# Moving a router's gate logits to VectorE and cutting expert units to 64 rows

## The chip, the cores and the metric

The kernel runs on one core of a Trainium2 chip. The metric is the time of one execution in device microseconds (us). A core has TensorE (PE, with PEld for its weight loads), VectorE (DVE), ScalarE (ACT), GpSimd (POOL) and SyncE (SP, which here only issues DMAs). Each engine works through its own list of instructions in order. It waits for the others by semaphores.

## The reference

Three layers follow each other. B = 2, H = 8, S = 768, D = 64, so there are 1536 tokens of 512 channels.

```python
scores = where(is_sink | in_window, q @ k.T / 8, -1e9)     # 4 sinks, window 128
x = softmax(scores) @ v                                     # attention
h = x @ w_in;  x = maximum(0.01 * h, h) @ w_out             # 512 -> 2048 -> 512, fp64 weights in
logits = x @ w_gate                                         # 512 -> 8 experts
expert = argmax(logits); gate = softmax(logits)[expert]
# each expert takes its first 384 tokens, the others' rows stay zero
out[token] = gate * (maximum(X[expert] @ w1[expert], 0) @ w2[expert])   # 512 -> 1024 -> 512
```

Of the 1536 tokens the experts 0 to 7 get 177, 257, 53, 101, 45, 4, 228 and 671 (the last is cut to 384).

## The kernel before

**Precision.** Every operand of a matmul is held as a high and a low part, and a product is the sum of three matmuls: high by high, high by low, low by high.

**Dense layers.** The tokens go in six blocks (j = 0 to 5) of 256, which is two tiles of 128 tokens. A block has 16 steps f, one for each 128 hidden channels. A step issues `first` (L1099, 12 matmuls of 256 columns into `hps`), a slice of the attention of later tiles, and the `second` of two steps before (L1147, 6 matmuls of 512 columns into `y`). Between the two lies the leaky ReLU: ACT L1117, DVE L1118 (`g`), and the split into `gp`. There are two `hps` buffers, so the `first` of step f+2 waits for the DVE `g` of step f. In block 0 the fp64 weights are also turned into fp32 by bit operations on VectorE ("words", L1010 to L1030), split into parts (`wl` on POOL, L1046) and stored. Later blocks read them from memory.

**Routing.** The router works on block j during block j+1. ACT L1224 copies the block's two `y` out as `x2`. `transpose` (L1233) turns them on TensorE by eight transposes (`xps`), and VectorE copies them out (`x2T`, L1235). `parts` (L1245, `kls`) and `logits` (L1258, `lps`) are ten small matmuls. Then come `place` (softmax, position in the expert's queue) and `scatter` (rows to the queues in memory). One of these calls is taken at each step of the tuple `ROUTE`.

**Experts.** `Experts` works through the experts by falling size, in seats: 0 to 3 are long (`group`), 4 is of one unit (`lone`), and 5 to 7 are of 64 rows (`half`). A unit is 128 rows. Seats 0 to 3 hold 384, 228, 177 and 257 rows, in the order 384, 228, 177, 257, thus 3, 2, 2 and 3 units. `group` first transposes the units after the first (L1617), working at the first ones' matmuls between (`up`, L1636, of one unit's 128 columns). Then the remaining matmuls of `up` run over all of the seat's columns, into four tiles `ph`. `h_parts` makes `ht` of them. `down` (L1685) takes 24 matmuls of 512 columns for each unit, and `out` scales and stores. In `half`, the high and low parts of 64 rows stand side by side in 128 columns, so that two matmuls do what three do elsewhere. The expert weights come by DMA as fp64 (`craw`), and ACT L1472 and DVE L1470 and L1474 make parts (`cw`) of them.

**Which path.** The number of units of each seat is known only when the counts are. The tuple `USUAL` names the expected numbers. If the counts agree, a path written out for them is run, and otherwise a general one with branches.

Of the kernel before, what the change touches and what calls it, by code (L numbers as in the profile page):

```python
# [18 lines left out]
P = 128  # L19
# [28 lines left out]
WORD_US = 0.6  # L48
PARTS_US = 2.0
ROUTE = (2, 4, 6, 9, 10, 11, 14)  # L50
HOLD, TAIL = 4, 1
# [377 lines left out]
class RingAttention(Attention):  # L429
# [298 lines left out]
    def pv_low(self, t, g):  # L728
        if (t, g) in self.lo:
            lo, hi, ps = self.lo.pop((t, g))  # L730
            self.pace.vector(0.4)
            self.nc.vector.tensor_tensor(out=lo, in0=ps, in1=hi.bitcast(F32), op=ALU.subtract)
# [218 lines left out]
class FFN:  # L951
# [198 lines left out]
class Router:  # L1150


    def __init__(self, nc, tc, pools, A, capacity, ident):
# [25 lines left out]
        self.lT = {}  # L1179
        nc.sync.dma_start(out=self.wg, in_=A["moe2_w_gate"].rearrange("(k p) e -> p k e", p=P))  # L1180

        self.before = c.tile([P, P], BF16, name="before")
# [45 lines left out]
    def transpose(self, ts):  # L1228
        nc = self.nc
        for t in ts:  # L1230
# [5 lines left out]
            self.xT[t] = xT  # L1236

    def parts(self, ts):

# [11 lines left out]
    def logits(self, ts):  # L1251
        nc, E, sm = self.nc, self.E, self.p["sm"]
        nt = len(ts)
        ps = self.p["ps"].tile([P, nt, E], F32, tag="att", name="lps")
        lT = self.lT.pop(ts, None)
        for n, t in enumerate(ts):
            if lT is not None:
# [123 lines left out]
class Experts:  # L1381
# [14 lines left out]
    PARTS = 50  # L1396
    USUAL = (3, 2, 2, 3)

    def __init__(self, nc, tc, pools, A, router, ident):
# [21 lines left out]
        self.tail = [gi for gi, (e, js) in enumerate(self.groups) if e >= self.short]  # L1421
        self.usual = self.USUAL if self.tail[0] == len(self.USUAL) == self.short else ()
        if self.usual:
            self.bounds = [self.p["const"].tile([P, self.short], F32, name=f"bound{a}") for a in range(2)]
            for (e, js), u in zip(self.groups, self.usual):
                nc.gpsimd.memset(self.bounds[0][:, e:e + 1], float((u - 1) * P + 1))
                nc.gpsimd.memset(self.bounds[1][:, e:e + 1], float(u * P if u < len(js) else 2 ** 20))

# [154 lines left out]
    def fetch(self, gi, n=0):  # L1583
# [4 lines left out]
        if gi < len(self.known):  # L1588
            for u in range(n, self.known[gi]):
                self.get(gi, u)  # L1590
            return
# [3 lines left out]
        if n < len(js):  # L1595
            with self.tc.If(self.csp[s] > js[n] * P):
                self.get(gi, n)
                if n + 1 < len(js):
                    self.fetch(gi, n + 1)

    def fetch_one(self, gi):
# [16 lines left out]

    def x_parts(self, gi, n, px):

        nc, DM = self.nc, self.DM
        h, l = (self.xt[:, a, :, n * P:(n + 1) * P] for a in range(2))
# [4 lines left out]
    def up(self, e, h, f, u0, u1):  # L1627

        nc = self.nc
        sl = slice(u0 * P, u1 * P)  # L1630
        mm = [(k, w, a) for k in range(self.K) for w, a in ((0, 0), (0, 1), (1, 0))]
# [7 lines left out]

    def h_parts(self, h, f, u, n):  # L1640

        nc = self.nc
        ps = self.ph[f][:, u * P:n * P]
        hh, hl = (self.ht[:, a, h * self.HF + f, u * P:n * P] for a in range(2))
        nc.scalar.activation(hh, ps, AF.Relu)
        nc.vector.scalar_tensor_tensor(out=hl, in0=ps, scalar=0.0, in1=hh.bitcast(F32), op0=ALU.max,
                                       op1=ALU.subtract)
# [27 lines left out]
    def down(self, e, h, n, turn=False, last=None):  # L1675
        nc = self.nc
        for f in range(self.HF):
# [6 lines left out]
            for m, (x, w) in enumerate(((hh, wh), (hh, wl), (hl, wh))):  # L1684
                nc.tensor.matmul(self.py[n], lhsT=x, rhs=w, start=(h == 0 and f == 0 and m == 0),  # L1685
                                 stop=(h == self.NH - 1 and f == self.HF - 1 and m == 2))

    def out(self, gi, n):
# [73 lines left out]

    def half_out(self, gi):
        nc, Q = self.nc, P // 2
        gt, ys, py = self.gt[gi % 4][0], self.ys[self.nout % 2], self.py[gi % 2]
        self.nout += 1
# [13 lines left out]
    def half(self, gi):  # L1780
# [22 lines left out]
        self.half_out(gi)  # L1803

    def group(self, gi, n, u0):

# [4 lines left out]
        nxt = gi + 1 < len(self.groups)  # L1811
        m = n - u0
        for u in range(u0 + (u0 == 0), n):
            px = self.px if (u - u0) % 2 == 0 else self.ph[3].rearrange("p (k c) -> p k c", k=self.K)
            if gi or u >= self.ready:
# [20 lines left out]
        for u in range(u0, n):  # L1836
            for h in range(self.NH):
                self.down(e, h, u)
                if u == n - 1:
                    self.release("b", gi, h)  # L1840
                    if h < self.NH - 1:
                        self.refill(self.PACE[2])
            self.out(gi, u)
        for h in range(0 if m > 0 else self.NH):
# [23 lines left out]
    def run(self):  # L1868
# [64 lines left out]
        with self.tc.If(self.off <= 0, preferred_fallthrough_block=True) as c:  # L1933
            self.known = self.usual + (1,) * len(tail)
            for gi, n in enumerate(self.usual):
                self.group(gi, n, int(gi == 0))
            self.known = ()
# [7 lines left out]
def build(tc, A, n_sink, window, capacity):  # L1945
# [14 lines left out]
    with ExitStack() as es:  # L1960
# [145 lines left out]

        pending, held, routing, splits = [], [], [], []
        n_ev = ffn.NF - ffn.CAP
        late = NB - 1

        def route(ts, ahead=False):
            return [lambda: rt.transpose(ts), *[lambda: rt.parts(ts)] * (ahead and rt.tiled), lambda: rt.logits(ts),
                    *[lambda: None] * (ahead and not rt.tiled), lambda: rt.place(ts),
                    *(lambda t=t: rt.scatter(t) for t in ts)]

        def split(n, f=-1, x=0):
# [5 lines left out]
        def second():  # L2122
# [23 lines left out]
            if last:  # L2146
                ts = tuple(range(j * TPB, (j + 1) * TPB))
                for t, y in zip(ts, ffn.y.pop(j)):
                    rt.evac(t, y)
                routing.extend(route(ts, True))  # L2150
                if j == late - 2 and rt.NU:
# [62 lines left out]
        rawst.close()  # L2214
        pool(es, "rt", bufs=2)
        for j in range(1, NB):
            need_t = TPB * (j + 2) - 1
# [3 lines left out]
            if j == late:  # L2221
                att.close()
# [113 lines left out]
```

## Time and profile before

| | |
|---|---|
| time, median of three executions | 570.53 us (570.47 to 570.69) |
| the profiled execution's own time | 570.18 us |
| its span, first to last instruction | 568.1 us |
| TensorE clock granted, mean | 0.998 |
| PE busy | 550.2 us (97%) |
| DVE busy | 341.0 us (60%) |
| ACT busy | 291.6 us (51%) |
| POOL busy | 186.4 us (33%) |
| DMA | 91.63 MB, mean 161 GB/s |

The span is 2.1 us shorter than the time of the same execution, since it leaves out what lies before the first and after the last instruction. An engine's share is an average over the whole span. The dense blocks 1 to 5 lie between about 100 and 395 us, the long seats between 400 and 517 us, and the short ones after them.

### The profile page before, as it was taken

The numbers are of one execution on the slowest core, as the hardware profiler recorded it, in microseconds if no ns is written. First come the engines' busy times: TensorE is split into PE (matmuls) and PEld (weight loads), VectorE is DVE, ScalarE is ACT, GpSimd is POOL, SyncE is SP. The second block draws the span as 40 slices with busy tenths as digits, with TensorE's granted clock in tenths as the row PEclk, the third lists the DMA queues.
The fourth block names the chain that finished last, engine by engine and source line by source line (L and its number), as shares of the span: only waits on it lengthen the run. The fifth ranks groups of instructions, "written<-read, shape, count | busy, mean of one in ns | idle before, by whom it ended". The sixth has DMA issues, their size and how long they took to land.

```text
span 568.1 us, 11287 instructions
## 1 busy us (share of the span) xinstructions
PE 550.2 (97%) x3801; PEld 472.4 (83%) x3801; DVE 341.0 (60%) x829; ACT 291.6 (51%) x859; POOL 186.4 (33%) x338
## 2 busy tenths in 40 slices
PE   8988999999999999999999999999999999999994
PEld 7777657888898888888888888887899898988783
DVE  6999995766443533444444522575577666637992
ACT  6767646765445545444444433453444443526771
POOL 5567679623422243224332322241202011001120
PEclk9999999999999999999999999999999999999999
DMA  9979865999242023402230157562487676437930
GB/s 232 239 230 278 272 217 164 312 254 344 81 125 80 20 75 94 113 20 64 70 99 2 40 159 246 170 208 68 148 263 244 199 221 194 148 120 213 315 104 9
DMA packets 83557, 91.63 MB, mean 161 GB/s; under 512 B 42980, under 2 KB 51172, under 8 KB 83489
## 3 DMA queue, kind: packets, MB, share of 16 engines
q1 hardware_dynamic: 81504, 85.68, 50.3%
q0 software_dynamic: 1984, 5.13, 2.6%
q8 instruction: 32, 0.52, 0.4%
q14 instruction: 37, 0.29, 0.2%
HBM read 72.01 MB, written 20.09 MB: 162 GB/s over the span
## 4 chain that ended last, share of the span: by engine, by line
PE 75%; DVE 8%; issue 6%; DMA 5%; POOL 2%; ACT 2%; SPq 0%; POOLq 0%; DVEq 0%; ACTq 0%
PE hps L1099 21%; PE y L1147 21%; PE ph L1636 10%; PE py L1685 9%; PE ops L713 3%; PE sps L617 2%; DMA craw<-in_moe_w 2%; DMA out<-ys,gt 2%; DVE word L1017 2%; DVE word L1021 2%; PE pps L675 1%; PE qps L564 1%; DMA rawo<-in_moe_w_out 1%; DVE cvt L1027 1%; PE xps L1233 1%
## 5 line engine op out<-in xcount | busy, mean ns | idle before, releaser
L1147 PE MATMUL y<-wh,gp 128*128 128x512 f32 x344 | 126.7, 409 | 0.9 <-ACT gp L1127 0.7
L1129 POOL TENSOR_TENSOR gp<-g,gp 128x256 fp32r<-128x256 f32 x77 | 57.2, 743 | 179.9 <-ACT gp L1127 163.6
L1118 DVE TENSOR_TENSOR g<-hps,g 128x256 f32<-128x256 f32 x80 | 33.7, 422 | 103.6 <-ACT g L1117 101.5
L1099 PE MATMUL hps<-xth,wh 128*128 128x256 f32 x320 | 91.9, 287 | 0.4 <-DVE g L1118 0.4
L1099 PE MATMUL hps<-xtl,wh 128*128 128x256 f32 x320 | 90.2, 282 | 0.0
L1099 PE MATMUL hps<-xth,wl 128*128 128x256 f32 x320 | 89.9, 281 | 0.0
L1474 DVE TENSOR_TENSOR cw<-craw,cw 128x512 fp32r<-128x512 f32 x128 | 83.1, 693 | 10.3 <-ACT cw L1472 8.1
L1147 PEld LDWEIGHTS y<-wh,gp 128*128 128x128 f32 x344 | 64.5, 188 | 16.0 <-ACT gp L1127 1.1
L1472 ACT CAST cw<-craw 128x512 fp32r<-128x512 f32 x112 | 63.3, 621 | 23.7 <-PE py L1685 23.0
L1117 ACT ACTIVATE g<-hps 128x256 f32<-128x256 f32 x80 | 30.6, 382 | 84.6 <-PE hps L1099 80.0
L1147 PE MATMUL y<-wl,gp 128*128 128x512 f32 x172 | 67.6, 393 | 0.0
L1685 PE MATMUL py<-cw,ht 128*128 128x512 f32 x264 | 64.1, 398 | 0.2 <-DVE ht L1673 0.2
L1099 PEld LDWEIGHTS hps<-xth,wh 128*128 128x128 f32 x320 | 60.3, 188 | 4.5 <-DVE g L1118 1.4
L1099 PEld LDWEIGHTS hps<-xtl,wh 128*128 128x128 f32 x320 | 60.2, 188 | 2.1
L1099 PEld LDWEIGHTS hps<-xth,wl 128*128 128x128 f32 x320 | 60.6, 189 | 0.0
L1685 PEld LDWEIGHTS py<-cw,ht 128*128 128x128 f32 x264 | 48.9, 188 | 11.8 <-DVE ht L1673 1.0
L1636 PE MATMUL ph<-xt,cw 128*128 128x256 f32 (+2 forms) x444 | 57.7, 290 | 0.1
L1636 PEld LDWEIGHTS ph<-xt,cw 128*128 128x128 f32 x444 | 56.5, 189 | 0.5 <-issue 0.3
L1694 POOL DMA_INDIRECT out<-ys,gt x11 | 11.1, 1007 | 112.8 <-DVE ys L1693 101.8
L1127 ACT CAST gp<-g 128x256 fp32r<-128x256 f32 x80 | 32.9, 411 | 21.6 <-DVE g L1118 20.2
L640 ACT ACTIVATE pm<-pm,mx 128x132 f32<-128x132 f32 (+1 forms) x80 | 31.9, 402 | 10.3 <-DVE mx L632 10.3
L1147 PEld LDWEIGHTS y<-wl,gp 128*128 128x128 f32 x172 | 32.5, 189 | 4.4 <-POOL wl L1046 0.3
(255 smaller groups left out, 993.1 us busy)
## 6 DMA issues: line engine op xcount, KB each, us to landing
craw<-in_moe_w SPq DMA_DIRECT2D x128, 256.0 KB
rawi<-in_moe_w_in SPq DMA_DIRECT2D x16, 512.0 KB
rawo<-in_moe_w_out SPq DMA_DIRECT2D x16, 512.0 KB
places<-zero SPq DMA_DIRECT2D x24, 257.0 KB
wh<-wscr SPq DMA_DIRECT2D x16, 256.0 KB
wl<-wscr SPq DMA_DIRECT2D x16, 256.0 KB
xg<-places SPq DMA_DIRECT2D x12, 257.0 KB
natv<-in_v SPq DMA_DIRECT2D x12, 256.0 KB
```

The source lines that it names most:

```text
L640: self.nc.scalar.activation(a, a, AF.Exp, bias=mx[:, pr, e:e + 1], accum_out=su[:, pr, e, 0:1])
L713: nc.tensor.matmul(ps[64 * e:64 * e + 64, pr, :], lhsT=l, rhs=r, start=(x == 0 and not (late and pr)), stop=(x == len(mm[0]) - 1 and not l ...
L1099: nc.tensor.matmul(ps, lhsT=w, rhs=x, start=(n == 0), stop=(n == len(mm) - 1))
L1117: nc.scalar.activation(g, ps, AF.Copy, scale=0.01)
L1118: nc.vector.tensor_tensor(out=g, in0=ps, in1=g, op=ALU.max)
L1127: nc.scalar.copy(gp[:, 0], g)
L1129: eng.tensor_tensor(out=gp[:, 1], in0=g, in1=gp[:, 0].bitcast(F32), op=ALU.subtract)
L1147: nc.tensor.matmul(y, lhsT=l, rhs=r, start=(start and n == 0), stop=(stop and n == len(mm) - 1))
L1472: nc.scalar.copy(h, t)
L1474: eng.tensor_tensor(out=l, in0=t, in1=h.bitcast(F32), op=ALU.subtract)
L1636: nc.tensor.matmul(self.ph[f][:, sl], lhsT=self.w[e, "a", h, k][w][:, f * P:(f + 1) * P], rhs=self.xt[:, a, k, sl], start=(m == 0), stop=( ...
L1685: nc.tensor.matmul(self.py[n], lhsT=x, rhs=w, start=(h == 0 and f == 0 and m == 0), stop=(h == self.NH - 1 and f == self.HF - 1 and m == 2))
```

## The change

There are four parts.

1. **Gate logits.** At the start of the loop for block 2, `start_rows` broadcasts the 512 x 8 gate to all partitions (`rows_of`, 128 x 4096 fp32). For blocks 1, 2 and 3 `products` forms the logits on VectorE: for each tile and expert one scalar_tensor_tensor of 128x512 that multiplies `x2` with the gate column and adds up along the row (`accum_out`). That is 16 for a block, two at each of eight steps. The calls that remain (`logits`, which only passes the sums on, `place`, two `scatter`) run one a step from step 9 on (`AFTER`). Blocks 0, 4 and 5 are routed as before.
2. **Low weights last.** In block 0, `first` takes the four matmuls with the low weights at the end and no longer at every third place.
3. **Units turned a seat ahead.** On the expected path `turn_ahead` transposes the units of the next seat between the two halves of the `down` of this seat's first unit, and `up` runs over all columns from its first matmul.
4. **Short last units.** `USUAL` counts half units of 64 rows. Where the last unit of a seat has at most 64 rows (seats 2 and 3), `up` leaves out 64 columns, high and low parts of `ht` stand side by side, and `down_short` takes 16 matmuls in place of 24. `h_parts` makes the low part in two DVE instructions, `get_short` reads in two DMAs, and `half_out` takes an ACT and a DVE instruction in place of a DVE one.

A changed constant in `pv_low` alters what the planner books for that operation. The lists of instructions show no move that comes from it.

```diff
+AFTER = range(9, 16)
-        mm = [(w[:, k, :], x[k]) for k in range(self.K) for w, x in mm]
+        mm = [(w[:, k, :], x[k]) for w, x in mm for k in range(self.K)] if j == 0 else \
+            [(w[:, k, :], x[k]) for k in range(self.K) for w, x in mm]
...
+    def start_rows(self):
+        self.rows_of = self.p["wgb"].tile([P, self.DM, self.E], F32, name="rows_of")
+        src = self.A["moe2_w_gate"].rearrange("(o d) e -> o (d e)", o=1)
+        self.nc.sync.dma_start(out=self.rows_of.rearrange("p d e -> p (d e)"),
+                               in_=src.to_broadcast([P, self.DM * self.E]))
+    def products(self, ts, n, es):
...
+        junk = self.p["c"].tile([P, DM], F32, tag="c", name="junk")
+        for e in es:
+            nc.vector.scalar_tensor_tensor(out=junk, in0=self.x2[ts[n]][:, 0:DM], scalar=1.0,
+                                           in1=self.rows_of[:, :, e], op0=ALU.mult, op1=ALU.mult,
+                                           accum_out=self.lg[ts][:, n, e:e + 1])
...
-    USUAL = (3, 2, 2, 3)
+    USUAL = (6, 4, 3, 5)
...
+        if cut:
+            w, q = (n - 1 - u) * P, n * P - cut
+            lo = self.ht[:, 0, h * self.HF + f, q:n * P]
+            nc.vector.scalar_tensor_tensor(out=lo, in0=ps[:, w:], scalar=0.0, in1=hh[:, w:].bitcast(F32), op0=ALU.max,
+                                           op1=ALU.subtract)
...
+    def down_short(self, e, h, n):
+        for f in range(self.HF):
+            for m, w in enumerate(self.w[e, "b", h, f]):
+                self.nc.tensor.matmul(self.py[n], lhsT=self.ht[:, 0, h * self.HF + f, n * P:(n + 1) * P], rhs=w,
...
-                    self.up(e, h, f, u0 + (h == 0 and f < m - 1), n)
-                    self.h_parts(h, f, u0, n)
+                    self.up(e, h, f, u0 + (not turned and h == 0 and f < m - 1), n, cut)
+                    self.h_parts(h, f, u0, n, cut)
...
-                self.down(e, h, u)
+                if cut and u == n - 1:
+                    self.down_short(e, h, u)
+                else:
+                    self.down(e, h, u)
+                if known and u == u0 and gi + 1 < self.short:
+                    self.turn_ahead(gi + 1, h + 1)
...
+            if ahead and rt.rows_of is not None and len(ts) == 2:
+                es = list(range(rt.E))
+                beside.extend(lambda n=n, e=e: rt.products(ts, n, es[e:e + PAIR])
+                              for n in range(len(ts)) for e in range(0, rt.E, PAIR))
+                return [lambda: rt.logits(ts), lambda: rt.place(ts), *(lambda t=t: rt.scatter(t) for t in ts)]
...
-                if routing and i in ROUTE:
+                if beside:
+                    beside.pop(0)()
+                elif routing and i in (ROUTE if rt.rows_of is None else AFTER):
```

The first place is VectorE's list in the first steps of block 2. `g` is the leaky ReLU, `ri` and the row sums before it belong to the softmax of the attention, `qT`, `kTl`, `xtl` and `vh` are other parts of the attention, and `x2T` is the copy for the router. The kernel before:

```order
L1118 TENSOR_TENSOR g<-hps,g 128x256
L648 TENSOR_REDUCE ri<-su_134 128x4
L649 RECIPROCAL ri<-ri 128x4
L1118 TENSOR_TENSOR g<-hps,g 128x256
L586 SCALAR_TENSOR_TENSOR qT<-qps,qT 128x256
L590 TENSOR_TENSOR kTl_130<-qps,kTh_129 128x2x128
L1235 COPY x2T<-xps 128x512 x2
L1118 TENSOR_TENSOR g<-hps,g 128x256
L732 TENSOR_TENSOR xtl<-ops,xth 128x2x128
```

The same stretch of VectorE's list now (`junk,rlg` is a product, at L1255 of the changed kernel):

```order
L1120 TENSOR_TENSOR g<-hps,g 128x256
L1255 SCALAR_TENSOR_TENSOR junk,rlg<-x_2526,rows_of 128x512 x2
L649 TENSOR_REDUCE ri<-su_134 128x4
L650 RECIPROCAL ri<-ri 128x4
L1120 TENSOR_TENSOR g<-hps,g 128x256
L587 SCALAR_TENSOR_TENSOR qT<-qps,qT 128x256
L591 TENSOR_TENSOR kTl_130<-qps,kTh_129 128x2x128
L1255 SCALAR_TENSOR_TENSOR junk,rlg<-x_2526,rows_of 128x512
L1120 TENSOR_TENSOR g<-hps,g 128x256
L1255 SCALAR_TENSOR_TENSOR junk,rlg<-x_2526,rows_of 128x512
L733 TENSOR_TENSOR xtl<-ops,xth 128x2x128
```

Two products now stand between one `g` and the next, ahead of the row sums or to either side of a `g`, and the copies `x2T` are gone.

The second place is TensorE's list from the end of seat 2 into the `up` of seat 3. `py` are the matmuls of `down`, `px` and `ph` out of `xg` the transposes, `ph` out of `xt` the `up`. The kernel before:

```order
L1685 MATMUL py_5869<-cw,ht 128x512 x24
L1617 MATMUL ph_5868<-ident,xg_1_4846 128x128 x4
L1636 MATMUL ph_5505<-xt,cw 128x128 x12
L1617 MATMUL px<-ident,xg_2_4847 128x128 x4
L1636 MATMUL ph_5506<-xt,cw 128x128 x12
L1636 MATMUL ph_5505<-xt,cw 128x256 x12
L1636 MATMUL ph_5506<-xt,cw 128x256 x12
L1636 MATMUL ph_5544<-xt,cw 128x384 x12
```

TensorE's list now (L1649 transposes, L1726 `down`, L1732 `down_short`, L1669 `up`):

```order
L1726 MATMUL py_5542<-cw,ht 128x512 x12
L1649 MATMUL ph_5541<-ident,xg_1_4843 128x128 x4
L1726 MATMUL py_5542<-cw,ht 128x512 x12
L1649 MATMUL ph_5865<-ident,xg_2_4844 128x128 x4
L1732 MATMUL py_5866<-cw,ht 128x512 x16
L1669 MATMUL ph_5502<-xt,cw 128x320 x12
L1669 MATMUL ph_5503<-xt,cw 128x320 x12
```

The transposes of seat 3 have moved into the `down` of seat 2, the split matmuls of 128 and 256 columns are gone, the full width is 320 in place of 384 columns, and the short unit's `down` has 16 matmuls.

## Rows read from the trace of the kernel before

**Rows 1.** Windows: busy us of PE, PEld, DVE, ACT, POOL; clock, DMA share, GB/s.

```profile
190.00:270.00 80.00, 80.00 (x622) 70.39 (x621) 36.24 (x113) 38.57 (x143) 27.27 (x42) 1.00 0.23 65
430.00:500.00 70.00, 70.00 (x464) 65.14 (x463) 45.08 (x80) 31.66 (x64) 7.13 (x12) 1.00 0.62 199
```

**Rows 2.** Chain of waits, block 4's routing: start, length, what.

```profile
343.79 1.43 PE hps L1099 x12
...
346.60 0.87 PE xps L1233 x8
...
353.10 0.57 PE kls L1245 x16
353.67 1.62 PE hps L1099 x12
...
359.47 0.34 PE lps L1258 x4
359.82 1.52 PE hps L1099 x12
```

**Rows 3.** Line L1021: ns min/median/max, starts, form.

```profile
L1021 DVE SCALAR_TENSOR_TENSOR word<-rawi,word x13: 685/689/694, 27.6 to 53.7; 128x512 int32<-128x512 int32 x13
...
L1021 DVE SCALAR_TENSOR_TENSOR cvt<-rawo,cvt x1: 1410/1410/1410, 18.0 to 18.0; 128x512 int32<-128x512 int32 x1
```

**Rows 4.** Line L1235: ns min/median/max, starts, form.

```profile
L1235 DVE COPY x2T<-xps x12: 676/681/694, 109.0 to 392.8; 128x512 f32<-128x512 f32 x12
```

**Rows 5.** Windows: block 3's stretch with the routing.

```profile
221.80:253.30 31.50, 31.50 (x250) 27.71 (x248) 14.73 (x45) 15.54 (x57) 9.10 (x17) 1.00 0.29 80
```

**Rows 6.** Timeline of VectorE: start, length, instruction.

```profile
240.21 0.42 DVE L1118 TENSOR_TENSOR g<-hps,g 128x256 f32<-128x256 f32 x1 [2.69 <-ACT g L1117]
```

**Rows 7.** Timeline of TensorE: the later user of that buffer.

```profile
245.07 0.37 PE L1099 MATMUL hps<-xth,wh 128*128 128x256 f32 x1
```

**Rows 8.** Timeline of SP's queue at block 2.

```profile
148.54 0.52 SPq L175 DMA_DIRECT2D natq<-in_q  x1
```

**Rows 9.** Timeline of ACT: a block's tiles copied out.

```profile
164.85 1.17 ACT L1224 COPY x<-y 128x512 f32<-128x512 f32 x2
```

**Rows 10.** Chain of waits, the long seats.

```profile
431.89 12.64 PE ph L1636 x108
...
444.97 11.19 PE py L1685 x48
...
481.27 1.29 PE ph L1636 x12
...
483.03 17.08 PE ph L1636 x108
```

**Rows 11.** Windows: the seats after the long ones.

```profile
517.30:530.00 12.70, 12.51 (x60) 9.92 (x60) 10.51 (x19) 9.37 (x18) 1.36 (x2) 1.00 0.98 288
540.00:550.20 10.20, 9.93 (x54) 8.23 (x53) 9.71 (x18) 8.19 (x16) 2.01 (x2) 1.00 0.38 127
```

**Rows 12.** Waits of TensorE, 517.3 to 560 us: total, times, longest.

```profile
PE py L1759 <- DVE ht L1752: 0.7, 2, 0.4
```

**Rows 13.** Timeline of VectorE: the last weight split.

```profile
556.15 0.69 DVE L1474 TENSOR_TENSOR cw<-craw,cw 128x512 fp32r<-128x512 f32 x1 [0.82 <-ACT cw L1472]
```

**Rows 14.** Timeline of TensorE: its reader.

```profile
556.75 3.51 PE L1759 MATMUL py<-cw,ht 128*128 128x512 f32 x14
```

**Rows 15.** Waits of TensorE, 30 to 60 us.

```profile
PE hps L1099 <- POOL wl L1046: 3.6, 5, 0.9
```

**Rows 16.** Windows: block 0.

```profile
20.00:90.00 70.00, 65.37 (x443) 48.45 (x444) 68.62 (x139) 44.20 (x142) 48.45 (x95) 1.00 0.75 229
```

**Rows 17.** Chain of waits, the end of block 0.

```profile
95.20 0.75 POOL gp L1129
...
95.99 1.20 PE y L1147 x4
```

More of the change, by code (lines that the diff above doesn't have):

```diff
@@ L1236, in transpose @@
             self.xT[t] = xT
+    def start_rows(self):
[4 more added lines that the diff above has]
+    def products(self, ts, n, es):
+        nc, DM = self.nc, self.DM
+        if ts not in self.lg:
+            self.lg[ts] = self.p["sm"].tile([P, len(ts), self.E], F32, tag="rsc", name="rlg")
+        junk = self.p["c"].tile([P, DM], F32, tag="c", name="junk")
[3 more added lines that the diff above has]
+                                           accum_out=self.lg[ts][:, n, e:e + 1])
     def parts(self, ts):
@@ L1253, in logits @@
         nt = len(ts)
-        ps = self.p["ps"].tile([P, nt, E], F32, tag="att", name="lps")
+        ps = self.lg.pop(ts, None)
+        done = ps is not None
+        if not done:
+            ps = self.p["ps"].tile([P, nt, E], F32, tag="att", name="lps")
         lT = self.lT.pop(ts, None)
-        for n, t in enumerate(ts):
+        for n, t in enumerate(() if done else ts):
             if lT is not None:
@@ L1421, in __init__ @@
         self.tail = [gi for gi, (e, js) in enumerate(self.groups) if e >= self.short]
-        self.usual = self.USUAL if self.tail[0] == len(self.USUAL) == self.short else ()
+        self.usual = self.USUAL if self.tail[0] == len(self.USUAL) == self.short and self.NH == 2 else ()
         if self.usual:
@@ L1588, in fetch @@
         if gi < len(self.known):
-            for u in range(n, self.known[gi]):
-                self.get(gi, u)
+            for u in range(n, -(-self.known[gi] // 2)):
+                (self.get_short if 2 * u + 1 == self.known[gi] else self.get)(gi, u)
             return
@@ L1599, in fetch, with get_short @@
                     self.fetch(gi, n + 1)
+    def get_short(self, gi, n):
+        s, js = self.groups[gi]
+        r = js[n] * P
+        src = self.r.queues[bass.ds(self.order[s], 1), r:r + P // 2, :].rearrange("e p c -> (e p) c")
+        for a in range(2):
+            self.nc.sync.dma_start(out=self.xg[gi % 2][n][a * (P // 2):(a + 1) * (P // 2), :], in_=src)
     def fetch_one(self, gi):
@@ L1617, in turn, with x_parts @@
             self.nc.tensor.transpose(px[:, k, :], x[:, k * P:(k + 1) * P], self.ident)
-    def x_parts(self, gi, n, px):
+    def x_parts(self, gi, n, px, cut=0):
         nc, DM = self.nc, self.DM
-        h, l = (self.xt[:, a, :, n * P:(n + 1) * P] for a in range(2))
+        h, l = (self.xt[:, a, :, n * P:(n + 1) * P - cut] for a in range(2))
+        px = px[:, :, 0:P - cut]
         nc.scalar.copy(h, px)
@@ L1638, in up, with h_parts @@
                              skip_group_check=True)
-    def h_parts(self, h, f, u, n):
+    def h_parts(self, h, f, u, n, cut=0):
         nc = self.nc
-        ps = self.ph[f][:, u * P:n * P]
-        hh, hl = (self.ht[:, a, h * self.HF + f, u * P:n * P] for a in range(2))
+        ps = self.ph[f][:, u * P:n * P - cut]
+        hh, hl = (self.ht[:, a, h * self.HF + f, u * P:n * P - cut] for a in range(2))
         nc.scalar.activation(hh, ps, AF.Relu)
+        if cut:
[3 more added lines that the diff above has]
+                                           op1=ALU.subtract)
+            ps, hh, hl = (t[:, 0:w] for t in (ps, hh, hl))
+            if not w:
+                return
         nc.vector.scalar_tensor_tensor(out=hl, in0=ps, scalar=0.0, in1=hh.bitcast(F32), op0=ALU.max,
@@ L1812, in group @@
         m = n - u0
+        known = gi < len(self.known)
+        cut = P // 2 * (known and self.known[gi] % 2)
+        turned = known and gi > 0
         for u in range(u0 + (u0 == 0), n):
+            if turned:
+                break
             px = self.px if (u - u0) % 2 == 0 else self.ph[3].rearrange("p (k c) -> p k c", k=self.K)
@@ L1842, in group @@
                         self.refill(self.PACE[2])
-            self.out(gi, u)
+            if cut and u == n - 1:
+                self.half_out(gi, u)
+            else:
+                self.out(gi, u)
         for h in range(0 if m > 0 else self.NH):
@@ L2105, in build @@
             ex.PARTS -= FEWER
-        pending, held, routing, splits = [], [], [], []
+        pending, held, routing, splits, beside = [], [], [], [], []
         n_ev = ffn.NF - ffn.CAP
@@ L2114, in route, with late_route @@
                     *(lambda t=t: rt.scatter(t) for t in ts)]
+        def late_route(ts):
+            rt.rows_of = None
+            return route(ts, True)
         def split(n, f=-1, x=0):
@@ L2149, in second @@
                     rt.evac(t, y)
-                routing.extend(route(ts, True))
+                routing.extend(route(ts, True) if j < late - 1 else late_route(ts))
                 if j == late - 2 and rt.NU:
@@ L2215, in build @@
         pool(es, "rt", bufs=2)
+        wgb = ExitStack()
         for j in range(1, NB):
+            if j == 2 < late and ring and rt.tiled and TPB == 2:
+                pool(wgb, "wgb", bufs=1)
+                rt.start_rows()
             need_t = TPB * (j + 2) - 1
```

30 lines of the change are left out of this document (21 added, 9 removed).

## The prediction, made before the changed kernel was run

> **What bounds the kernel now.** I read the windows first. In the dense blocks (190 to 270 us) TensorE is busy for 80.00 of 80 us at clock 1.00, and VectorE for 36.24. In the long seats (430 to 500 us) TensorE is busy for 70.00 of 70 and VectorE for 45.08 [rows 1]. So work taken off TensorE in these two stages shortens the span by its own length, as long as the work put on VectorE fits into the idle half. The reader is to see from this that the share of 60% for VectorE over the whole span is not what counts, but the room in the steps where the products fall. Next I read the chain of waits around one block's routing and in the seats, for what each piece costs on TensorE [rows 2, 10]. Then I read how long a buffer freed by VectorE lies ready before its next user [rows 6, 7], and at last block 0 and the short seats, where TensorE is not full.
>
> **Logits, what goes.** In the chain, eight transposes `xps` take 0.87 us. The `kls` matmuls take 0.57, and the 12 `hps` matmuls behind them take 1.62 where they otherwise take 1.43. The `lps` take 0.34, and the `hps` behind them 1.52 [rows 2]. That is 0.87 + (0.57 + 0.19) + (0.34 + 0.09) = 2.06 us for a block, and 6.2 us for the three blocks. These rows are of block 4, whose routing issues the same instructions.
>
> **Logits, what comes.** No row shows a product: a scalar_tensor_tensor of 128x512 whose second source steps by 32 bytes and which adds up along the row. The nearest rows are scalar_tensor_tensor of 128x512 with two SBUF sources, one of them stepping by 8 bytes, at 0.689 us (median), and once 1.410 us [rows 3]. That is 0.69 from below and 1.41 from above. For a fixed part, `g` of 256 columns takes 0.42 [rows 6], so 256 columns more cost 0.27 and the fixed part is about 0.15. An operation at half the rate would then take 0.15 + 2 x 0.53 = 1.22, at a third 1.75, at a quarter 2.29 (estimates).
>
> What VectorE can bear is read in the stretch of block 3 in which the routing lies: it is busy 14.73 of 31.50 us [rows 5]. Without two copies `x2T` at 0.68 [rows 4] that is 13.4, and the stretch shrinks to 29.4 us. So there are 16.0 us for the 16 products, which is 1.0 us each before a queue builds up. Behind a product that is late stands the next `g` on VectorE, and for that `g` waits the first matmul two steps later. The tightest `g` that I found in this stretch ends at 240.21 + 0.42 = 240.63, and the user of its buffer starts at 245.07 [rows 6, 7]. The slack is 4.4 us. So a block loses 16p - 16.0 - 4.4 us at a product price of p, and nothing below p = 1.28. At 0.69 and at 1.22 alike the loss is nothing, so I need not choose between them. I allow 0.1 us a block, 0.3 in all, for single matmuls that come late. At 1.41 a block loses 2.2, three lose 6.5.
>
> [...]
>
> The broadcast of the gate is 128 x 4096 x 4 = 2.1 MB. It stands in SP's queue behind the load of `natq` at 148.54 [rows 8], and at 288 GB/s, as in a stretch where the DMA share is 0.98 [rows 11], it takes 7.3 us. The first product can't start before ACT has copied the block's tiles out, from 164.85 on [rows 9]. It is there by about 157, and only the `natv` behind it in the queue comes some us later, for a tile that is used a block later. Cost: none. If the cover failed, the first products would wait, and the slack of 4.4 us would take that up. `place` and `scatter` move a few steps later in the same block. Nothing needs their rows before the experts, at 395 us. Cost: none.
>
> **Experts.** The `up` of the second seat takes 12.64 us for 24 matmuls of 128 columns and 84 of 256 [rows 10]. With 1.43 / 12 = 0.119 for 256 columns [rows 2], the 24 take 2.64, or 0.110 each. Now there are 96 of 256 columns, 11.4 us, which is 1.2 less. The third seat has the same list before (12.65 in the same chain) and now 96 matmuls of 192 columns, priced between 0.110 and 0.119. I take 11.0, which is 1.6 less. The fourth takes 1.29 + 17.08 = 18.37 [rows 10]. Less 24 of 128 at 0.110 and 24 of 256 at 0.119 there remain 12.9 us for 72 of 384, 0.179 each. Now there are 96 of 320 columns. Half way between 0.119 and 0.179 is 0.149, or 14.3 us, 4.1 less (bounds: 7.0 to 1.2 less). The `down` of two units takes 11.19 for 48 [rows 10], 0.233 each, and two short units save 8 each: 3.7 us. Sum: 1.2 + 1.6 + 4.1 + 3.7 = 10.6 us.
>
> The number of transposes is the same. They lie a `down` earlier, so the parts made from them are ready well before `up` starts, and the split that covered them is not missed. The 16 added DVE instructions, the two DMAs of 64 rows and the extra ACT step of the output lie beside a TensorE that is full, on engines with a third or more of the stage free (VectorE 45.08 of 70, ACT 31.66 [rows 1]). Without that cover the 16 would cost some 16 x 0.22 = 3.5 us (the fixed part of 0.15 and 64 columns).
>
> What is late next: the weights of the short seats. From 517 us on VectorE is busy 10.51 of 12.7 us with a DMA share of 0.98, and 9.71 of 10.2 later on [rows 11]. TensorE still waits only 0.7 us there [rows 12]. The last split of weights starts at 556.15 and the run of matmuls that ends with its user at 556.75 takes 3.51 [rows 13, 14]. So there are about 2.8 us of lead (with 0.69 for the split). TensorE comes to these seats 10.6 us earlier, but what frees the buffers for the loads comes earlier as well. I take 0.5 us for it; bounds are 0 and half of the gain, 5.3.
>
> **Block 0.** TensorE waits 3.6 us in five places for `wl` [rows 15], the operand that now comes last. VectorE is busy 68.62 of the 70 us from 20 to 90 us with the words [rows 16], and at the end of the block it is POOL's `gp` that releases the `y` matmuls [rows 17]. So what TensorE gains at 35 to 53 us it waits for later. I take 0; bounds are 0 and -3.6.
>
> **Sum.** -6.2 + 0.3 - 10.6 + 0.5 - 0 = -16.0. The profiled execution took 570.18 (568.1 of span and 2.1 around it), and would take 554.2. The median of the runs lies 0.35 above it, so I predict 554.3, between the two.
>
> **Rivals.**
> - *Half price.* A product costs some 1.4 us. For it: the row of 1.410 and the unknown accumulator. Against: it stands once, beside 13 at 0.685 to 0.694 [rows 3]. Time: 554.2 + 6.5 = 560.7.
> - *VectorE becomes the bound of blocks 2 to 4 (slower).* The step of 32 bytes and the sum along the row slow the product together, to a third or a quarter of the rate. At 1.75 a block loses 7.6 us and the time is 554.2 + 22.8 = 577. At 2.29 a block loses 16.2 and it is 603. It decides from the price at which three blocks lose 16.0: (5.3 + 20.4) / 16 = 1.61 us. For it: no row has either property. Against: a step of 8 bytes costs nothing, 0.689 against 0.68 of a plain copy [rows 3, 4].
> - *The short seats' weights take back half of the experts' gain.* For it: VectorE and DMA are nearly full there [rows 11]. Against: TensorE's waits are short [rows 12]. Time: 554.2 + 4.8 = 559.
> - *The experts' new path isn't taken*, and the gain is that of the logits alone: 570.2 - 5.9 = 564.3, or above 570 if the general path is slow. For it: 257 rows stand at the lower edge of 257 to 320. Against: the edge was 257 before, and 228 and 177 lie inside 193 to 256 and 129 to 192.
> - *Block 0's waits come off.* Time: 554.2 - 3.6 = 550.6.
>
> **How the numbers follow.** Forecast 0.62, half price 0.12, short seats 0.11, block 0 0.05, path not taken 0.03, VectorE the bound 0.07. A measurement can tell about 0.2% (1.1 us) from no change. The first four are faster, and most of the fifth: 0.92 faster, 0.01 the same, 0.07 slower. The forecast's own range is 552 to 556.5, from the bounds of the fourth seat's `up` (-2.9, +2.9) with not all of either end. Block 0 takes the range down to 550, half price and short seats up to 561. Outside are the path not taken and VectorE as the bound, 0.10.
>
> **What would show it.** In the profile after, a product's mean below 1.28 us and TensorE busy without gaps in blocks 2 to 4, with blocks shorter by 2 us each. The `up` of the last three long seats at about 11.4, 11.0 and 14.3 us, the short units' `down` at 16 x 0.233. The waits for `wl` gone but block 0 as long as before. TensorE's waits from the short seats' weights below 1.5 us. I am wrong if the product takes 1.6 us or more, if the idle time of TensorE before `hps` grows in blocks 2 to 4, or if the short seats begin earlier by 16 us and end earlier by far less.

## The result and the profile after

The changed kernel takes 553.26 us (median, 552.72 to 554.03), the one before beside it 570.51. The ratio is 0.9704, with a 95% interval of 0.969 to 0.9717. That is 17.3 us less. 554.3 was predicted, from a sum of 16.0 less than the profiled execution of before. The profiled execution after took 553.2 us, its span is 551.5.

The two spans are cut at the starts of ACT's copies of a block's two tiles (L1224 before, L1227 after) and at the seats:

| stage | before us | after us | difference |
|---|---|---|---|
| to the end of block 0 | 104.06 | 103.40 | -0.7 |
| block 1 | 60.79 | 60.75 | 0.0 |
| blocks 2, 3, 4 | 59.91, 61.13, 57.81 | 58.11, 59.47, 56.03 | -5.2 |
| block 5 and seat 0, to its `down` | 76.6 | 77.1 | +0.5 |
| long seats from there to their end | 97.0 | 85.9 | -11.1 |
| short seats, to the last matmul | 43.0 | 43.0 | 0.0 |

First the windows after, with the columns of [rows 1]: dense blocks, long seats, the stretch of block 3 in which the products run, and the seat after the long ones.

```profile
190.00:270.00 80.00, 79.90 (x600) 70.50 (x599) 60.00 (x161) 40.46 (x152) 35.88 (x44) 1.00 0.23 65
430.00:500.00 70.00, 70.00 (x433) 63.19 (x432) 46.38 (x100) 32.78 (x67) 7.45 (x10) 1.00 0.62 200
222.20:251.40 29.20, 29.20 (x219) 25.86 (x218) 28.69 (x62) 12.85 (x46) 16.91 (x16) 1.00 0.26 72
...
500.70:513.40 12.70, 12.51 (x61) 9.91 (x60) 11.74 (x21) 11.63 (x22) 1.18 (x2) 1.00 0.96 304
```

TensorE is as full as in [rows 1], and with less to do it is done earlier. VectorE went from 36.24 to 60.00 us in the dense window. While the products run in block 3 it is busy for 28.69 of 29.20 us, against 14.73 of 31.50 in [rows 5]. The average of 60.00 of 80 hides this. GpSimd, whose work is the same, went from 27.27 to 35.88. The last row answers to the first of [rows 11]: TensorE's 12.51 us are the same, though VectorE is fuller.

The products by line, with columns as in [rows 3]: the multiplication, and the reading of its sum, a second instruction that the list of instructions didn't show:

```profile
L1255 DVE SCALAR_TENSOR_TENSOR junk<-x,rows_of x48: 1106/1204/1717, 164.8 to 310.6; 128x512 f32<-128x512 f32 x48
L1255 DVE DVE_READ_ACCUMULATOR junk<-x,rows_of x48: 70/84/119, 166.0 to 311.8; 128x1 f32 x48
```

The chain of waits in the long seats, which answers to [rows 10]:

```profile
426.41 11.52 PE ph L1669 x96
...
449.96 10.70 PE ph L1669 x96
...
467.54 3.73 PE py L1732 x16
471.27 14.08 PE ph L1669 x96
...
496.98 3.73 PE py L1732 x16
500.71 3.64 PE ph L1697 x16
```

The `up` of the second to fourth seat (x96) and the two short `down` (x16) stand one after the other, with only transposes and other `down` between. There is no wait. The x96 also show that the expected path was taken.

### The profile page after: what moved, and what is told of

The parts are those of the page before. It is cut to its first block, busy times and chain, and to the rows that moved or that the text cites. A ratio compares the mean times of both kernels' runs of the same rounds, so it can differ in the third digit from the quotient of the medians.

```text
span 551.5 us, 11104 instructions
## 1 busy us (share of the span) xinstructions
PE 534.3 (97%) x3653; PEld 457.8 (83%) x3653; DVE 393.6 (71%) x935; ACT 291.4 (53%) x858; POOL 209.8 (38%) x338
## 5 line engine op out<-in xcount | busy, mean ns | idle before, releaser
L1131 POOL TENSOR_TENSOR gp<-g,gp 128x256 fp32r<-128x256 f32 x77 | 66.4, 862 | 151.1 <-ACT gp L1129 128.5
L1496 ACT CAST cw<-craw 128x512 fp32r<-128x512 f32 x112 | 63.4, 620 | 17.6 <-PE py L1732 9.2
L1255 DVE SCALAR_TENSOR_TENSOR junk<-x,rows_of 128x512 f32<-128x512 f32 x48 | 63.0, 1312 | 1.2 <-ACT x L1227 1.0
L1726 PE MATMUL py<-cw,ht 128*128 128x512 f32 x216 | 53.7, 400 | 0.2 <-DVE ht L1714 0.2
L1669 PE MATMUL ph<-xt,cw 128*128 128x256 f32 (+3 forms) x396 | 49.9, 287 | 0.5 <-DVE ht L1687 0.5
L1669 PEld LDWEIGHTS ph<-xt,cw 128*128 128x128 f32 x396 | 49.5, 189 | 1.1 <-DVE ht L1687 0.7
L1726 PEld LDWEIGHTS py<-cw,ht 128*128 128x128 f32 x216 | 39.6, 188 | 9.4 <-DVE ht L1714 1.0
L1742 POOL DMA_INDIRECT out<-ys,gt x9 | 9.8, 1084 | 93.3 <-DVE ys L1741 84.0
```

The source lines that it names most:

```text
L1131: eng.tensor_tensor(out=gp[:, 1], in0=g, in1=gp[:, 0].bitcast(F32), op=ALU.subtract)
L1255: nc.vector.scalar_tensor_tensor(out=junk, in0=self.x2[ts[n]][:, 0:DM], scalar=1.0, in1=self.rows_of[:, :, e], op0=ALU.mult, op1=ALU.mult, ...
L1496: nc.scalar.copy(h, t)
L1669: nc.tensor.matmul(self.ph[f][:, sl], lhsT=self.w[e, "a", h, k][w][:, f * P:(f + 1) * P], rhs=self.xt[:, a, k, sl], start=(m == 0), stop=( ...
```

## The experiments

**The parts alone.** Part 1 alone keeps the changed kernel's products and puts back the order of block 0 (with the constant in `pv_low`) and the seats:

```diff
...
-    USUAL = (6, 4, 3, 5)
+    USUAL = (6, 4, 4, 6)
...
-        turned = known and gi > 0
+        turned = False
...
-                if known and u == u0 and gi + 1 < self.short:
+                if False:
```

> Part 1 alone (block 0 and the seats as before). My theory: the gain of the parts adds up, and the logits give what the three blocks lost between the traces, 5.2 us: 565.3 us, blocks 2 to 4 each 1.7 to 1.8 us shorter, block 0 and the seats as before. Rival: the seats alone would give the whole of the gain over the bound, since the work put on VectorE in blocks 2 to 4 delays something that only shows later: under 3 us of gain, 568 or more.

Measured: 564.94 us, ratio 0.9911 (0.9897 to 0.9925), thus 5.2 us less than before (570.13 on that chip). Blocks 2 to 4 take 58.12, 59.41 and 56.06 us, as in the changed kernel.

The seats alone, without products and with the old order in block 0:

```diff
...
-            if j == 2 < late and ring and rt.tiled and TPB == 2:
+            if j == 2 > late and ring and rt.tiled and TPB == 2:
```

> Parts 3 and 4 alone (logits on TensorE, block 0 as before). My theory: the seats give 11.1 us and the short seats behind them take nothing back: 559.4 us. Rival (weights of the short seats late): that part of the gain of the seats came only because the blocks before were shorter, or it is taken back behind them: 562 or more, with waits of TensorE for ht or cw over 1.5 us after the long seats.

Measured: 559.05 us, ratio 0.9806 (0.9794 to 0.9819), 11.1 us less. TensorE's waits from seat 0 to the end are these (waited for, total, times, longest):

```profile
PE py L1806 <- DVE ht L1799: 0.7, 2, 0.4
PE py L1725 <- DVE ht L1713: 0.2, 1, 0.2
```

They are the 0.7 of [rows 12] and the same 0.2 that was there before, so the short seats take nothing back. The rival of late weights falls.

The turning alone, with units of 128 rows, no products and the old order in block 0:

```diff
...
-    USUAL = (6, 4, 3, 5)
+    USUAL = (6, 4, 4, 6)
...
-                nc.gpsimd.memset(self.bounds[0][:, e:e + 1], float((u - 1) * P // 2 + 1))
+                nc.gpsimd.memset(self.bounds[0][:, e:e + 1], float((u - 2) * P // 2 + 1))
...
```

> Part 3 alone: units turned a seat ahead, all units of 128 rows, so up has 96 matmuls of full width in seats 1 to 3 and down is as before. My theory: 96 matmuls of 256, 256 and 384 columns, 11.4, 11.4 and 17.2 us in place of 12.6, 12.6 and 18.4: 3.6 us of gain, 566.9 us. Rival: the transposes a seat ahead cost as much elsewhere, since ACT and VectorE make their parts in the middle of down: no gain, 570.5.

Measured: 566.62 us, ratio 0.9937 (0.9925 to 0.9949), 3.5 us less, so the rival falls. The `up` of the three seats in its chain:

```profile
432.54 11.39 PE ph L1668 x96
...
455.99 11.52 PE ph L1668 x96
...
479.99 16.90 PE ph L1668 x96
```

12.64, 12.65 and 18.37 became 11.39, 11.52 and 16.90, which is 3.9 us. So of the 11.1 us about a third comes from fewer, wider matmuls. The rest is put down to the units of 64 rows, which were not run alone.

The order in block 0 alone is part 2 (with the constant in `pv_low`) put into the kernel before.

> Part 2 alone (and the changed booking in pv_low): low weights last in block 0. My theory: TensorE waits less for wl and more for the attention's parts behind VectorE, and 0.0 to 0.7 us remain: 569.9 to 570.5 us. Rival: the 3.6 us of waits for wl come off: 567.

Measured: 569.52 us, ratio 0.9992 (0.9982 to 1.0002), which is no change that can be told. TensorE's waits in block 0 (24 to 104 us) there, which answer to [rows 15]:

```profile
PE hps L1100 <- ACT wh L1045: 1.9, 3, 0.9
PE sps L617 <- DVE xtl L732: 0.8, 1, 0.8
PE hps L1100 <- POOL wl L1046: 0.5, 3, 0.2
PE pps L675 <- DVE pm L627: 0.4, 1, 0.4
PE y L1148 <- POOL gp L1130: 0.2, 1, 0.2
```

The 3.6 us for `wl` became 0.5. In their place TensorE waits 1.9 us for the high weights and 1.2 for the attention's parts from VectorE, of which 0.3 was there before. The rival of 567 falls. The end of block 0 also varies between the profiled executions of kernels that are alike there, from 103.1 to 105.1 us, so the -0.7 of the table can't be put down to the order.

**What a product costs, and why.** The first of the next runs puts operations without use beside the products, in three kinds by turns. This leaves the products as they are and adds VectorE time. `step` is a gate column in steps of 32 bytes, `line` are 512 consecutive numbers:

```diff
...
+        if kind == 0:
+            nc.vector.scalar_tensor_tensor(out=junk, in0=x, scalar=1.0, in1=step, op0=ALU.mult, op1=ALU.mult)
+        elif kind == 1:
+            nc.vector.scalar_tensor_tensor(out=junk, in0=x, scalar=1.0, in1=line, op0=ALU.mult, op1=ALU.mult)
+        else:
+            nc.vector.scalar_tensor_tensor(out=junk, in0=x, scalar=1.0, in1=line, op0=ALU.mult, op1=ALU.mult,
+                                           accum_out=self.lg[ts][:, n, es[0]:es[0] + 1])
```

> All parts, and beside every two products one more VectorE operation of 128x512, of three kinds in turn, whose result is not used: second source in steps of 32 bytes without a sum; second source without steps, without a sum; without steps, with a sum. Theory A (the sum along the row costs the second pass): 0.7, 0.7 and 1.2 us. Theory B (the step of 32 bytes does): 1.2, 0.7 and 0.7 to 0.8. Either way a block gets 8 operations of 0.87 on average, so by the sum of the prediction (a block loses what 16 products of 1.31 and these 7.0 exceed 16.0 + 4.4) each of three blocks loses 7.5 us: 576. Rival (VectorE's queue is no limit there, other waits are): 556 or less.

Measured: 575.49 us. The three kinds by line (the last with the reading of its sum):

```profile
L1257 DVE SCALAR_TENSOR_TENSOR junk<-x,rows_of x8: 1081/1262/1716, 166.4 to 321.2; 128x512 f32<-128x512 f32 x8
...
L1259 DVE SCALAR_TENSOR_TENSOR junk<-x,rows_of x8: 673/684/1227, 171.3 to 327.1; 128x512 f32<-128x512 f32 x8
...
L1261 DVE SCALAR_TENSOR_TENSOR junk<-x,rows_of x8: 670/688/1087, 176.8 to 331.5; 128x512 f32<-128x512 f32 x8
L1261 DVE DVE_READ_ACCUMULATOR junk<-x,rows_of x8: 73/77/95, 177.4 to 332.5; 128x1 f32 x8
```

A step of 32 bytes costs with and without a sum (minimum 1081 without, and 1084 for the products in the same run, which have one). Without a step the sum costs nothing but its reading of 0.08 us (670 against 673). Theory B holds, and theory A falls. Blocks 2 to 4 take 65.30, 66.81 and 63.14 us, 7.2 us more each. 7.5 was expected. But only part of it is waiting: TensorE's waits in the three blocks are 14.2 of the 21.6 us. Three windows of block 2, with columns as in [rows 1]:

```profile
185.00:195.00 10.00, 6.21 (x47) 4.98 (x47) 9.96 (x21) 3.96 (x15) 5.94 (x6) 1.00 0.12 27
195.00:205.00 10.00, 10.00 (x56) 8.68 (x56) 9.86 (x25) 2.98 (x12) 1.84 (x3) 0.83 0.01 2
205.00:215.00 10.00, 10.00 (x85) 8.73 (x84) 6.38 (x25) 6.06 (x25) 4.69 (x7) 1.00 0.30 80
```

TensorE idles for 3.8 us while VectorE is full (9.96 of 10). In the window behind that its granted clock is 0.83, and the six `y` matmuls from 195.94 on take 2.6 us, where four groups of six in the chain of the kernel before (228 to 245 us) take 1.36 to 1.58. That the gap lowers the clock isn't shown: block 0 has gaps at a clock of 1.00 [rows 16]. Over the three blocks the clock is 0.97, 0.95 and 0.97 in windows of 67, 67 and 63 us, which makes 7.3 us lost (an estimate). That is about what the waits leave over.

The second takes other steps, again beside the products; `flat` is the whole gate in a row, so that `0:2 * DM:2` is a step of 8 bytes:

```diff
...
+        if kind == 0:
+            nc.vector.scalar_tensor_tensor(out=junk, in0=x, scalar=1.0, in1=flat[:, 0:2 * DM:2], op0=ALU.mult, op1=ALU.mult)
+        elif kind == 1:
+            nc.vector.scalar_tensor_tensor(out=junk, in0=x, scalar=1.0, in1=flat[:, 0:4 * DM:4], op0=ALU.mult, op1=ALU.mult)
+        else:
+            nc.vector.scalar_tensor_tensor(out=junk, in0=x, scalar=1.0, in1=flat[:, 0:3 * DM:3], op0=ALU.mult, op1=ALU.mult)
```

> All parts, and beside every two products one operation of 128x512 without a sum, whose second source goes in steps of 8, 16 and 12 bytes in turn; the result is not used. Theory A (any step over 8 bytes reads at half the rate): 0.69, 1.2, 1.2 us. Theory B (each step of 16 bytes opens a new piece of memory, smaller steps share one): 0.69 at 8, 1.2 at 16, and between the two at 12. Theory C (only far steps cost): 0.69 for all three. The time is 573 to 577 us, as with the three kinds before.

Measured: 576.17 us. The steps of 8, 16 and 12 bytes by line:

```profile
L1257 DVE SCALAR_TENSOR_TENSOR junk<-x,rows_of x8: 673/787/1237, 164.5 to 320.5; 128x512 f32<-128x512 f32 x8
...
L1259 DVE SCALAR_TENSOR_TENSOR junk<-x,rows_of x8: 1066/1080/1640, 168.8 to 325.8; 128x512 f32<-128x512 f32 x8
...
L1261 DVE SCALAR_TENSOR_TENSOR junk<-x,rows_of x8: 837/882/1571, 174.8 to 330.6; 128x512 f32<-128x512 f32 x8
```

The minima are 673, 1066 and 837 ns, as theory B has it, and neither A (1.2 us at 12 bytes) nor C (0.69 throughout). Why the steps cost this, no run shows. The medians are in part higher: of the 24 operations 19 ran beside one of GpSimd (last section).

**Where VectorE becomes the bound.** Every product issued twice:

```diff
-        for e in es:
+        for e in [e for e in es for _ in range(2)]:
```

> Every product is issued twice. My theory (VectorE becomes the bound beyond 20.4 us a block): 32 x 1.31 - 20.4 = 21.5 us a block lost, 64 in all: 618 us, with TensorE waiting before hps for VectorE's g. Rival (room in the later steps takes it up): under 590.

Measured: 604.27 us, ratio 1.0596 (1.0577 to 1.0615). Blocks 2 to 4 take 77.11, 75.32 and 72.42 us, which is 19.0, 15.8 and 16.4 more than in the changed kernel. TensorE's waits between 95 and 420 us:

```profile
PE sps L618 <- DVE kTl L591: 15.4, 3, 5.2
PE pps L1317 <- DVE roh L1298: 7.3, 3, 2.8
PE pps L676 <- DVE pm L628: 5.6, 3, 2.0
PE sps L618 <- DVE xtl L733: 2.7, 4, 0.7
PE kps L680 <- DVE pm L628: 1.8, 2, 0.9
PE hps L1101 <- DVE g L1120: 0.8, 2, 0.4
```

The limit is there, and VectorE sets it. The size was 13 us too high (51 in place of 64). Part of it is the price, 1.24 us on average here, which gives 19.3 a block. But the waits are only 33.6 us, 11.2 a block, so the queue held up TensorE by far less than the sum says. The rest goes with the clock again:

```profile
164.00:242.00 78.00, 65.85 (x432) 56.20 (x431) 61.46 (x147) 30.50 (x110) 24.97 (x31) 0.91 0.20 54
242.00:317.00 75.00, 64.51 (x445) 55.82 (x444) 61.00 (x146) 28.55 (x107) 26.37 (x32) 0.91 0.20 53
317.00:390.00 73.00, 61.96 (x417) 53.70 (x416) 56.93 (x138) 24.04 (x82) 25.52 (x30) 0.93 0.21 64
```

A clock lower by 0.09, 0.09 and 0.07 over 78, 75 and 73 us makes 18.9 us (an estimate), and 51.2 of blocks less 33.6 of waits leaves 17.6. Why the queue had more room than worked out stays open. The place was wrong too: nearly all the waits are for the attention's parts and the routing's own, and only 0.8 us are for `g`, from which the slack had been worked out.

**Products for block 0 as well.** The broadcast is issued a block earlier:

```diff
-            if j == 2 < late and ring and rt.tiled and TPB == 2:
+            if j == 1 < late and ring and rt.tiled and TPB == 2:
```

> Products for block 0 too (the broadcast one block earlier). My theory: one more block gives its 1.7 us: 551.5 us. Rival: the work that VectorE and POOL still have in block 1 (the last weights) leaves less room, and the block loses what it gains: 553.3 or more.

Measured: 559.45 us, ratio 0.9818 (0.9797 to 0.9839), about 6 us more than the changed kernel. The profiled execution is one of the longer two of five (561.72). In it block 1 takes 69.4 us in place of 60.75. The first product on VectorE, and the window of block 1 just behind it:

```profile
110.42 1.18 DVE L1255 SCALAR_TENSOR_TENSOR junk<-x,rows_of 128x512 f32<-128x512 f32 x1 [3.90 <-DMA rows_of<-in_moe_w_gate]
```

```profile
115.00:125.00 10.00, 8.19 (x39) 7.11 (x40) 9.87 (x24) 4.72 (x16) 2.18 (x2) 0.66 1.02 311
```

The broadcast is late: it is issued at 99.41 us, and the product could start at 106.5. In the changed kernel it is issued 17 us before its first product and takes 9.1. Here it takes some 11, with a DMA share of 1.04 from 95 to 105 us and 0.98 from 105 to 115, so the early product is the larger cause and the full DMA engines the smaller. VectorE stands in front of the product for 3.90 us, and everything behind it waits. Then VectorE is full (9.87 of 10), as it still has some of the last weights in this block. TensorE has gaps (it is busy for 8.19 of 10), and its granted clock is 0.66 on average in this window. The rival held. How much of the loss is the late broadcast and how much the missing room, this run doesn't show.

**Rows of consecutive numbers.** The gate turned by a transfer of single numbers:

```diff
...
-                                           in1=self.rows_of[:, :, e], op0=ALU.mult, op1=ALU.mult,
+                                           in1=self.rows_of[:, e, :], op0=ALU.mult, op1=ALU.mult,
...
+                nc.sync.dma_start(out=rt.by_e, in_=A["moe2_w_gate"].rearrange("d e -> e d"))
```

> The gate is brought into rows of 512 consecutive numbers by a transfer during block 1, so that a product's second source has no steps. Theory A (the sum costs): products stay at 1.2 us, 553.3 us. Theory B (the step costs): products at 0.7 to 0.8, VectorE has room again, and the 0.2 to 0.3 us that each of three blocks still loses go: 552.6 us. Rival: the transfer of 4096 single numbers holds up other loads, 554 or more.

Measured: 584.53 us, ratio 1.0238 (1.0223 to 1.0254). The rival held, and by far more than it said. In SP's queue the transfer and what came behind it, and then TensorE's wait:

```profile
100.11 0.82 SPq L2302 DMA_DIRECT2D by_e<-in_moe_w_gate  x1
101.22 29.32 SPq L1057 DMA_DIRECT2D wscr<-wh  x1
```

```profile
PE y L1149 <- ACT wh L1046: 26.7, 1, 26.7
```

The store of `wh` behind the transfer took 29.32 us in the queue. ACT's next `wh` waited 32.8 us for that store, and TensorE 26.7 for ACT. But blocks 2 to 4 take 57.87, 59.08 and 55.69 us, 1.0 less in sum than in the changed kernel, as theory B said. So the rows were made on the chip:

```diff
...
+    def turn_gate(self):
+        ps = self.p["ps"].tile([self.E, self.K, P], F32, tag="att", name="gps")
+        for k in range(self.K):
+            self.nc.tensor.transpose(ps[:, k, :], self.wg[:, k, :], self.ident)
+        gT = self.p["c"].tile([self.E, self.DM], F32, tag="c", name="gT")
+        self.nc.scalar.copy(gT, ps.rearrange("e k c -> e (k c)"))
+        self.nc.sync.dma_start(out=self.by_e, in_=gT)
...
```

> As the kernel with rows of consecutive numbers, but these are made on the chip late in block 1 (four transposes of the gate on TensorE, one copy on ACT, a store of 16 KB), in place of the transfer of single numbers. My theory: blocks 2 to 4 give the 0.9 us that they gave there, the four transposes cost up to 0.4: 552.3 to 552.9 us, products at 0.77 us. Rival: the transposes hold up block 1 by more than that, or the products' room was no limit: 553.3 or more.

Measured: 553.52 us, which is the rival's side. Blocks 2 to 4 are 1.0 us shorter and block 1 is 0.45 longer (61.20), but block 0 was 1.4 longer in the profiled execution, with the same code. Since the other comparison had been made on another chip, both were run on one chip:

> The changed kernel once more, as the comparison on one chip for the run beside it: 553.3 us.

> The rows of consecutive numbers made on the chip, beside the changed kernel on one chip. My theory: blocks 2 to 4 are 0.9 to 1.0 us shorter and block 1 0.4 to 0.5 longer, so 0.5 us less than the run beside it, which the medians may just show; block 0 is the same code and only varies. Rival: the 1.4 us that block 0 was longer in the run before comes from the change: 0.5 us or more above the run beside it.

Measured: 553.33 us (553.04 to 554.15) for the changed kernel, 553.21 (552.64 to 553.5) with the rows made on the chip. Their profiled spans are 551.3 and 551.1. The 1.4 us of block 0 is gone (103.32 against 103.36), and the stages show the -0.9 and +0.4. The sum of 0.5 expected can't be told from nothing, and the rival falls. The products there:

```profile
L1264 DVE SCALAR_TENSOR_TENSOR junk<-x,rows_of x48: 673/684/1165, 165.1 to 308.4; 128x512 f32<-128x512 f32 x48
```

They take little more than half of before (median 684 ns in place of 1204). It brings the 0.9 us of blocks 2 to 4 and no more, since with few exceptions VectorE was not what ended last.

## Why the prediction was right

- *What bounds.* TensorE was full before and after in the blocks and the seats, so a removed instruction gave its length. The parts run alone give 5.2, 11.1 and 0.6 us, together 16.9 of the 17.3; the 0.6 can't be told from nothing.
- *Logits, what goes.* 2.06 a block was forecast. Summed up by the distance from each matmul to the next, blocks 2 to 4 lose 2.37 (`xps`), 1.72 (`kls`), 1.08 (`lps`) and 0.88 at the `hps` behind them: 6.05 against 6.2.
- *Logits, what comes.* This is the term that was too small: 0.3 was allowed, and about 0.74 us came, all at the `sps` matmuls of the attention. With cheaper products these 0.74 go (-0.53 and -0.20 at the two kinds of `sps`), which shows that VectorE's queue is their cause. `place` and `scatter` and the broadcast cost nothing that shows.
- *The price.* Taken as between 0.69 and 1.41, with no loss below 1.28. The mean of 1.312 and a reading of 0.08, part of which overlaps, lie on the edge of the room, and just over the 1.28 that was named as the sign. By the sum a block loses 16 x 1.31 - 20.4 = 0.6, and 0.25 was lost. Beyond the edge the room was right in part by luck: 7.2 a block came where it gave 7.5, but 4.7 of them were waits and about 2.4 the lower clock (an estimate from 0.97, 0.95 and 0.97), which the sum doesn't have. With every product twice it was 11.2 of waits where it gave 21.5. That the queue would hit `g` first was wrong; the attention's parts are tighter.
- *The rows behind the price.* The `word` rows at 0.689 do not have two SBUF sources, as the prediction says: the kernel puts `word` into PSUM, into the pools of TensorE's `hps` and `y`. Two SBUF sources have the four `cvt` rows of that line, at 0.681, 0.691, 0.986 and 1.410. The two long ones ran beside GpSimd's `pm` (last section). So the row on which the rival of half price stood fits another cause, the same that goes with products of 1.36 in place of 1.19.
- *Seats.* 1.2, 1.6, 4.1 and 3.7 were forecast. From the chains: 12.64 to 11.52 (1.1), 12.65 to 10.70 (1.95), 18.37 to 14.08 (4.3), and 16 x 0.233 (3.7). Half way between 256 and 384 columns was a good guess for 320: 14.08 / 96 = 0.147.
- *Late next.* 0.5 was taken for the short seats' weights and 0.0 came there. But seat 0 gave back 0.5 in the changed kernel, with a wait of 0.5 us for its `ht` from VectorE. That wait isn't there with the seats alone, and it is with part 1 alone. So the term fits by luck, at another place.
- *Block 0.* 0 was taken, and -0.6 to -0.7 measured, which lies within the scatter of that block. That other waits take the place of those for `wl` was foreseen.
- *The rivals.* VectorE as the bound needed 1.61 us; the price came to within 0.3 of that. Had the sum along the row slowed the product as well, down to a quarter of the rate (2.29 by the prediction's estimate), VectorE would have been the bound. No run shows such a price for the sum: without a step it took 670 ns with it and 673 without, and a reading of 0.08 us.

## What to carry to other kernels

Work taken off a full engine is worth its length only as long as the engine that takes it over has room in those very steps (here 6.05 us of TensorE's went and 0.74 came back): read its busy time in the stretch, not over the span, and work out from which price on it becomes the bound. Then look at which of its readers has the least slack, of all of them and not only of the one that comes to mind. A cheaper instruction on an engine that is hardly ever last buys hardly anything: here a product's median of 0.684 in place of 1.204 us brought 0.9 us in three blocks. And where a full engine begins to wait, look at its granted clock as well: in the two runs with added VectorE work, a third of TensorE's loss goes with it (7.3 of 21.6 us and 18.9 of 51.2, both estimates from the clocks of the windows). Do not let an engine's list meet an instruction whose data come by a DMA that was issued only shortly before: here that held VectorE for 3.90 us.

## What the runs showed of the hardware

In these traces, operations of VectorE and GpSimd with two sources in SBUF took longer where they ran beside each other. Of the 48 products, the 14 that overlap no `gp` and no `pm` of GpSimd (operations with two sources) take 1.19 us on average (1.16 to 1.22). The 34 others take 1.36, and up to 1.72. GpSimd's `gp` takes 0.75 where it overlaps no product (54) and 1.13 on average where it does (23). The same two and a half microseconds on both engines, first VectorE:

```profile
238.77 1.16 DVE L1255 SCALAR_TENSOR_TENSOR junk<-x,rows_of 128x512 f32<-128x512 f32 x1
...
239.97 1.62 DVE L1255 SCALAR_TENSOR_TENSOR junk<-x,rows_of 128x512 f32<-128x512 f32 x1
```

```profile
238.77 1.76 POOL L1131 TENSOR_TENSOR gp<-g,gp 128x256 fp32r<-128x256 f32 x1 [4.47 <-ACT gp L1129]
```

The first product ends at about 239.85, when the next instruction starts on VectorE. If `gp` could only start then, it ran from 239.85 to 240.53, which is 0.68 (0.74 is the median). If the second product could only start at 240.53, it ran to 241.59, which is 1.06, about as long as the shortest (1.11). So by this estimate the pair fits operations that ran one after the other, with the waiting inside each record; one pair doesn't prove it, and no run tests it. With the rows made on the chip, without a step, both lose less: products take 0.70 free (14) and 0.80 beside GpSimd (34), and `gp` 0.95. The kernel before shows longer times too, where both sources of an operation of VectorE lie in SBUF, first VectorE:

```profile
17.97 1.41 DVE L1021 SCALAR_TENSOR_TENSOR cvt<-rawo,cvt 128x512 int32<-128x512 int32 x1
```

```profile
17.77 2.51 POOL L911 TENSOR_TENSOR pm<-pm,ri 128x512 f32<-128x512 f32 x2 [1.75 <-ACT pm L888]
```

The 28 `word` operations of the same line, whose second source lies in PSUM, take 0.674 to 0.694, though 13 of them ran beside GpSimd's `wl`. The `cvt` of 0.986 us, at 11.19, ran beside a `pm` from 10.67 to 11.63; the two that overlap no such operation take 0.681 and 0.691. No wait of TensorE is listed from 110 to 345 us of the changed kernel, so what GpSimd loses there costs nothing that shows; what the products lose is 0.12 us of their mean of 1.31.

With steps of 8, 12, 16 and 32 bytes in VectorE's second source, the shortest of eight operations of 128x512 took 673, 837, 1066 and 1081 ns, and without a step 673. And behind a transfer of 4096 single numbers the next store took 29.32 us in the queue, and TensorE waited for 26.7.
